# Reciprocals by Ln and Exp, and rows reversed by a transfer, in a fused linear-attention and state-space kernel

## The chip, the cores and the metric

The kernel runs on one core of a Trainium2 chip. A core has five engines that run side by side, each with its own in-order instruction queue: TensorE (PE, matrix products; PEld is its weight load), VectorE (DVE), ScalarE (ACT, which evaluates functions from a loaded table), GpSimd (POOL) and SyncE (SP), from which nearly all transfers of this kernel are issued. The engines wait for each other with semaphores. The metric is the device time of one execution in microseconds; a median of several runs is given.

## What is computed

Two independent parts, whose results stand side by side in one output of 2048 x 896.

Part A is linear attention with 16 heads of 28 over 2048 rows, whose features are softmaxes of a projection and of its negative:

```python
phi_q = concatenate([softmax(pq), softmax(-pq)])     # pk and phi_k alike
kv  = einsum("bhsf,bhsd->bhfd", phi_k, v)
z   = einsum("bhsf->bhf", phi_k)
num = einsum("bhqf,bhfd->bhqd", phi_q, kv)
den = einsum("bhqf,bhf->bhq", phi_q, z)[..., None] + 1e-6
o   = (num / den) @ wo
```

Part B convolves each of 448 columns of u (2048 rows) with a kernel that a diagonal state-space model with 256 states defines:

```python
P = exp(dt * A * l)                       # l = 0 .. 2047, A complex
K = einsum("dn,dnl,dn->dl", C, P, dt * B).real
y = irfft(rfft(pad(u)) * rfft(pad(K)))[:L] + u * Dskip
```

## The kernel before

Every operation is first recorded by a helper as a closure with its engine (`prog.add`), in the order of the code, and then issued in the order of a list of numbers, `ORDER` (1034 of them). So the program's text gives the numbers, and `ORDER` alone gives the order on each engine. Three more lists go with it: `PLACES` gives each buffer its place in one large SBUF tile `sbuf`, so buffers share bytes when their lives don't meet; `SLOTS` gives each product its PSUM banks; `PICKS` says for each copy, scaling or square (`copy`, `scaled`, `square`, lines 209, 212, 215) whether ACT or DVE does it: 228 letters, 17 of them V. Because of the helpers most instructions carry a helper's line: `mms` (L224) for products, `tt` (L181) for two-operand work on DVE, `af` (L202) for functions on ACT, `dma` (L244) and `dma_t` (L240, a transposing load) for transfers.

The stages, in the order in which they are recorded:

- Loads on SP: `log_dt`, the constants `PID` (six 128 x 128 matrices: the identity times 1, 3, 5, 7 and -1, and an anti-identity `REV`), six coefficient matrices of 224 KB (`load_raw`; one of them goes by ACT's queue), sixteen transposing loads of x (`load_x`), the weights, the DFT table `G1` (1 MB), and u.
- u is loaded by `load_u` (lines 274 to 276, with `row_pairs`, L267) in four transfers of 448 KB. A partition of the tile `ua[b]` holds pairs of neighbouring rows: index 0 of the pair is an even row and index 1 an odd row of u, 1792 contiguous bytes.
- Coefficients: step sizes on the diagonal (`DG`, and `DGN`, its negative by `scaled`), products with them, powers by Exp, cos and sin by Sin (`amp`, `cs`, `PW`), then `CB`, `K0`.
- `signal_spectrum(b)` (line 412) for the two halves b of u. The odd rows have to be in reversed order: four products per half with `REV` (L417, two recorded operations of two) give them in PSUM, two copies (L419) bring them to the tile `ur`; then a sum and a difference on DVE (L420, L421) give `ab`, and 64 products of 448 columns per half with `G1` (L434) give the spectrum, which goes to the DRAM tile `SUd`.
- `tables(qt)` for four quarters of the columns: angles by Sin (`rotations`), dampings by Exp (`dampings`), long products on DVE (`far`, `hi_tables`), 128 x 104 products in four column groups (`build_k`), and a rearrangement through the DRAM tile `KTd`.
- `key_side` (line 600) over eight pairs of row tiles: key features by Exp, their sums `bz` in PSUM, then a reciprocal on DVE (L620, `recip`, L198), written as bf16 into `VR`, and a multiplication of the values with it on DVE, which feeds the next products.
- `query_side(sc)` (line 637) over four row blocks: features, denominators, a reciprocal `R` (L664) of a 128 x 64 tile on DVE, a multiplication, a trip through the DRAM tile `SCd`, the output products and stores.
- `kernel_spectrum(qt)` and `conv(qt)`: products of spectra on DVE, inverse products on PE, eviction by ACT, stores.

Where two operations touch the same bytes (an SBUF place, a bank, a DRAM tile) the framework puts a semaphore wait in front of the second; a transfer's wait stands on the engine that issues it, and what is behind it on that engine's queue waits too. ACT's function tables are loaded by the compiler in front of an activation whose function the present table lacks.

Of the kernel before, what the change touches and what calls it, by code (L numbers as in the profile page):

```python
# [9 lines left out]
BF16 = mybir.dt.bfloat16  # L10
# [7 lines left out]
D_MODEL = 448  # L18
# [33 lines left out]
def _dft_tables():  # L52
# [24 lines left out]
    pid = np.zeros((128, 6, 128))  # L77
    for i, p in enumerate(ODD + [-1]):
        pid[np.arange(128), i, np.arange(128)] = p
    pid[np.arange(128), 5, 127 - np.arange(128)] = 1.0  # L80
# [43 lines left out]
def kernel(  # L124
# [23 lines left out]
    KTd = dram.tile([4, 3, 128, D_MODEL], BF16, name="KTd")  # L148
    SCd = dram.tile([4, 128, 128], BF16, name="SCd")
# [36 lines left out]
    def add(o, a, b):  # L186
        tt(o, a, b, ALU.add)
# [7 lines left out]
    def recip(o, a):  # L195
        def fn():
            with nc.allow_low_precision(reason="bf16 softmax weights, as in the reference"):
                nc.vector.reciprocal(o, a)  # L198
        prog.add("V", fn)

    def af(o, a, fn, **kw):
        prog.add("A", lambda: nc.scalar.activation(o, a, fn, **kw))  # L202
# [39 lines left out]
    def dma(eng, o, i):  # L242
        e = {"S": nc.sync, "G": nc.gpsimd}[eng]
        prog.add(eng, lambda: e.dma_start(out=o, in_=i))  # L244

    PID = sb([128, 6, 128])
# [3 lines left out]
    REV = PID[:, 5, :]  # L250
# [16 lines left out]
    def row_pairs(row, a):  # L267
        rs = u2.ap[0][0]
        return bass.AP(tensor=u2.tensor, offset=u2[row + 128 * (1 - a), 0].offset,
                       ap=[[2 * rs, 64], [256 * rs, 4], [1, 2 * D_MODEL]])  # L270

    ua = [sb([128, 4, 2, D_MODEL]) for _ in range(2)]

    def load_u(b):
        for a in range(2):
            dma("S", ua[b][64 * a:64 * a + 64].rearrange("p t r d -> p t (r d)"), row_pairs(1024 * b, a))
# [28 lines left out]
    dma("S", G1, G_d)  # L305
    load_u(0)
# [105 lines left out]
    def signal_spectrum(b):  # L412
        ab = sb([128, 2, 4, D_MODEL])
        ur = sb([128, 4, D_MODEL])
        for tp in range(2):
            bs = prog.banks(2)
            mms([(psum[:, bs[k], 0:D_MODEL], REV, ua[b][:, 3 - 2 * tp - k, 1, :], dict(start=True, stop=True))  # L417
                 for k in range(2)])
            copy(ur[:, 2 * tp:2 * tp + 2, :], two(bs))  # L419
        add(ab[:, 0], ua[b][:, :, 0, :], ur)  # L420
        sub(ab[:, 1], ua[b][:, :, 0, :], ur)  # L421
# [178 lines left out]
    def key_side():  # L600
        bK = prog.banks(1), prog.banks(1)
        for pr in range(8):
# [17 lines left out]
            recip(VR[:, :, :, D_HEAD, :], psum[:, bz, 0:64].rearrange("p (t s h) -> p t s h", t=2, s=2))  # L620
# [16 lines left out]
    def query_side(sc):  # L637
# [26 lines left out]
        recip(R, zz)  # L664
# [213 lines left out]
).split()]  # L878
PLACES = [64 * int(i) for i in (
# [52 lines left out]
```

## Time and profile before

| | |
|---|---|
| median of 3 runs | 236.51 us (236.47 to 238.96) |
| the profiled execution: its time, its span | 238.8 us, 237.1 us |
| instructions of PE, DVE, ACT | 3087, 263, 347 |
| table loads on ACT | 8 |
| transfers of u by `load_u` | 4 of 448 KB, issued from 5.25 us on |
| data moved by DMA | 36.99 MB in 82240 packets |
| granted clock of TensorE, mean | 0.985 |

A span reaches from the first to the last instruction; the execution's own time has a little more around it. Busy times are the time in which an engine has an instruction at work; matmuls are pipelined and their ends are modelled, so PE's is only rough. The idle time before an instruction is put down to what released it. The DMA share is the busy time of packets on the core's 16 DMA engines, as a share of all 16; packets that overlap on one engine can bring it above 1.

### The profile page before, as it was taken

To read this page: it belongs to the slowest core of one execution; us is meant where nothing else is said; L and a number is where in the kernel's file an instruction comes from. 1 tells how busy PE (TensorE), PEld (TensorE's weight loads), DVE (VectorE), ACT (ScalarE), POOL (GpSimd) and SP (SyncE) were. 2 spreads that over 40 slices of the span, in tenths; PEclk is the share of its full clock that TensorE was granted. 3 is DMA by queue.
4 is the path that set the end of the run, shared out by engine and by line. 5 is a ranking of instruction groups with operands and counts; after the bars stand their busy time and mean duration, and the time that the engine had idled before them with its cause. 6 is when DMAs were issued, how large, how long until landed. Compare 5 with 4: busy or idle time off the path is not lost.

```text
span 237.1 us, 7240 instructions
## 1 busy us (share of the span) xinstructions
PE 206.1 (87%) x3087; PEld 151.0 (64%) x3094; DVE 207.4 (87%) x263; ACT 191.7 (81%) x347; POOL 6.5 (3%) x21
## 2 busy tenths in 40 slices
PE   1448889999999899999999878499999969999991
PEld 1334435656548546687867867455579958779991
DVE  1899999999997799999999977589999996898950
ACT  3999999999999799999999999289756815935522
POOL 2000000000000100002000000000000000000000
PEclk9999999999999999999999999799999997999999
DMA  6999921849347786758266859907854990489395
GB/s 155 227 206 313 255 47 49 235 81 266 116 96 134 88 191 146 148 74 205 80 133 105 208 144 264 215 17 158 196 198 124 184 278 12 81 174 203 74 244 118
DMA packets 82240, 36.99 MB, mean 156 GB/s; under 512 B 65440, under 2 KB 80288, under 8 KB 81824
## 3 DMA queue, kind: packets, MB, share of 16 engines
q1 hardware_dynamic: 81968, 36.30, 70.4%
q8 instruction: 24, 0.39, 0.7%
q10 hardware_dynamic: 240, 0.23, 0.3%
q14 instruction: 8, 0.07, 0.1%
HBM read 20.04 MB, written 8.62 MB: 121 GB/s over the span
## 4 chain that ended last, share of the span: by engine, by line
PE 57%; ACT 6%; issue 5%; DMA 4%; DVE 4%; SPq 3%; ACTq 0%; POOL 0%; DVEq 0%; POOLq 0%
PE psum L224 57%; DVE sbuf L181 4%; ACT sbuf L209 3%; DMA sbuf<-SCd 3%; ACT sbuf L202 2%; SPq L244 2%; DMA out_dram<-sbuf 2%; SPq L240 1%; ACT sbuf L212 0%; ACT sbuf L215 0%; ACTq L927 0%; DVE sbuf L198 0%; PE psum L234 0%; POOL sbuf L219 0%; DVE sbuf L193 0%
## 5 line engine op out<-in xcount | busy, mean ns | idle before, releaser
L224 PE MATMUL psum<-sbuf 128*128 128x112 bf16 (+9 forms) x3051 | 204.7, 267 | 25.5 <-issue 6.8
L181 DVE TENSOR_TENSOR sbuf<-sbuf 128x896 bf16<-128x896 bf16 (+12 forms) x218 | 189.6, 936 | 16.6 <-ACT sbuf L202 4.4
L224 PEld LDWEIGHTS <-sbuf 128*128 128x128 bf16 (+4 forms) x3058 | 149.0, 116 | 79.8 <-issue 27.0
L209 ACT CAST sbuf<-psum 128x448 bf16<-128x448 f32 (+6 forms) x145 | 87.5, 675 | 29.5 <-PE psum L224 24.8
L202 ACT ACTIVATE sbuf<-psum 128x448 bf16<-128x448 f32 (+4 forms) x110 | 65.8, 755 | 0.0
L209 ACT COPY sbuf<-psum 128x192 f32<-128x192 f32 (+4 forms) x28 | 12.2, 470 | 6.1 <-PE psum L224 4.8
L215 ACT ACTIVATE sbuf<-sbuf 128x896 bf16<-128x896 bf16 (+1 forms) x16 | 16.5, 1098 | 0.7 <-DVE sbuf L181 0.7
L202 ACT ACTIVATE sbuf<-psum,sbuf 128x896 f32<-128x896 f32 (+3 forms) x17 | 13.3, 832 | 0.0
L202 ACT ACT_TABLE_LOAD x8 | 10.3, 1283 | 2.8 <-issue 1.5
L219 POOL MEMSET sbuf<- 128x224 bf16 (+6 forms) x16 | 6.0, 404 | 152.2 <-PE psum L224 142.0
L212 ACT ACTIVATE sbuf<-sbuf 128x896 bf16<-128x896 bf16 (+2 forms) x7 | 7.3, 1045 | 1.0 <-DVE sbuf L303 0.8
L209 ACT COPY sbuf<-sbuf 128x224 bf16<-128x224 bf16 (+2 forms) x14 | 7.3, 532 | 0.0
L198 DVE RECIPROCAL sbuf<-psum 128x64 bf16<-128x64 f32 x8 | 4.4, 552 | 2.1 <-ACT sbuf L209 1.9
L209 DVE CAST sbuf<-psum 128x448 bf16<-128x448 f32 (+1 forms) x5 | 4.0, 821 | 1.7 <-PE psum L224 1.7
L181 DVE TENSOR_TENSOR sbuf<-psum,sbuf 128x448 bf16<-128x448 f32 (+2 forms) x10 | 4.8, 498 | 0.6 <-ACT sbuf L209 0.6
L212 DVE TENSOR_SCALAR sbuf<-sbuf 128x896 bf16<-128x896 bf16 (+1 forms) x7 | 3.3, 490 | 0.0
L234 PE MATMUL psum<-sbuf 112*112 112x112 bf16 (+1 forms) x36 | 2.7, 216 | 0.4 <-DVE sbuf L181 0.4
L234 PEld LDWEIGHTS <-sbuf 112*112 112x112 bf16 (+1 forms) x36 | 2.4, 128 | 1.1 <-DVE sbuf L181 0.6
L198 DVE RECIPROCAL sbuf<-sbuf 128x64 f32<-128x64 f32 x4 | 2.2, 544 | 0.0
L193 DVE SCALAR_TENSOR_TENSOR sbuf<-sbuf 128x64 f32<-128x64 f32 (+1 forms) x5 | 1.9, 376 | 0.0
L209 ACT CAST sbuf<-sbuf 128x1792 bf16<-128x1792 f32 x1 | 1.8, 1793 | 0.0
L202 ACT ACTIVATE sbuf<-sbuf 112x4 bf16<-112x4 bf16 x1 | 0.2, 206 | 1.4 <-DMA sbuf<-in_B_log_dt_dram 1.4
(9 smaller groups left out, 3.4 us busy)
## 6 DMA issues: line engine op xcount, KB each, us to landing
sbuf<-SCd SPq DMA_DIRECT2D x16, 256.0 KB, 5.0
SUd<-sbuf SPq DMA_DIRECT2D x8, 448.0 KB, 3.9
sbuf<-SUd SPq DMA_DIRECT2D x4, 896.0 KB, 8.4
sbuf<-const SPq DMA_DIRECT2D x3, 1024.0 KB
sbuf<-const SPq DMA_DIRECT2D x8, 384.0 KB, 4.7
sbuf<-in_B_u_dram SPq DMA_DIRECT2D x4, 448.0 KB
out_dram<-sbuf SPq DMA_DIRECT2D x4, 448.0 KB, 4.1
out_dram<-sbuf SPq DMA_DIRECT2D x16, 112.0 KB, 3.7
```

Of the source, the lines that this page charges most:

```text
L181: prog.add("V", lambda: nc.vector.tensor_tensor(out=o, in0=a, in1=b, op=op))
L193: prog.add("V", lambda: nc.vector.scalar_tensor_tensor(out=o, in0=a, scalar=s, in1=b, op0=op0, op1=op1))
L198: nc.vector.reciprocal(o, a)
L202: prog.add("A", lambda: nc.scalar.activation(o, a, fn, **kw))
L209: either(lambda: nc.scalar.copy(o, a), lambda: nc.vector.tensor_copy(o, a))
L212: either(lambda: nc.scalar.activation(o, a, ACT.Copy, scale=s), lambda: nc.vector.tensor_scalar_mul(o, a, s))
L215: either(lambda: nc.scalar.activation(o, a, ACT.Square), lambda: nc.vector.tensor_tensor(out=o, in0=a, in1=a, op=ALU.mult))
L219: prog.add("G", lambda: nc.gpsimd.memset(o, v))
L224: nc.tensor.matmul(o, lhsT=l, rhs=r, **kw)
L234: nc.tensor.transpose(o, i, idn)
L240: prog.add("S", lambda: nc.sync.dma_start(out=o, in_=i, transpose=True))
L244: prog.add(eng, lambda: e.dma_start(out=o, in_=i))
```

## The change

Three parts, with all four lists made anew.

`recip` becomes two activations on ACT, the natural logarithm into a new F32 tile and then Exp with scale -1. It is called twelve times: eight in `key_side`, four in `query_side`. `af` now loads the table set `natural_log_exp_and_others` itself before the first Exp or Ln that follows a Sin (or nothing), so that one set serves both.

The anti-identity goes (`PID` has five matrices), and with it the eight products and the four copies of `signal_spectrum`. Instead one transfer, `reverse_u`, copies the odd rows of u in reversed order into a new DRAM tile `URd`, and `load_u` makes eight loads of 224 KB: the even rows from u into `ue`, the reversed odd rows from `URd` into `ur`.

`ORDER` has 1043 numbers, `PICKS` 224 letters, 26 of them V. SP's order begins: `log_dt`, five coefficient loads, `reverse_u`, the even rows of half 0 (two loads), `PID`, the first load of reversed rows of half 0, a part of `w_phi`, the second load, `G1`, then loads of x, the rest of u, the weights.

```diff
-    pid = np.zeros((128, 6, 128))
+    pid = np.zeros((128, 5, 128))
...
-    pid[np.arange(128), 5, 127 - np.arange(128)] = 1.0
...
+    URd = dram.tile([2, 512, D_MODEL], BF16, name="URd")
...
-    def recip(o, a):
-        def fn():
-            with nc.allow_low_precision(reason="bf16 softmax weights, as in the reference"):
-                nc.vector.reciprocal(o, a)
-        prog.add("V", fn)
+    def recip(o, a, t):
+        af(t, a, ACT.Ln)
+        af(o, t, ACT.Exp, scale=-1.0)
+
+    table = [None]
 
     def af(o, a, fn, **kw):
-        prog.add("A", lambda: nc.scalar.activation(o, a, fn, **kw))
+        def issue():
+            want = fn if fn == ACT.Sin else ACT.Exp
+            if want == ACT.Exp and table[0] != want:
+                nc.scalar.preload_act_table_set("natural_log_exp_and_others")
+            table[0] = want
+            nc.scalar.activation(o, a, fn, **kw)
+        prog.add("A", issue)
...
-    def row_pairs(row, a):
-        rs = u2.ap[0][0]
-        return bass.AP(tensor=u2.tensor, offset=u2[row + 128 * (1 - a), 0].offset,
-                       ap=[[2 * rs, 64], [256 * rs, 4], [1, 2 * D_MODEL]])
-
-    ua = [sb([128, 4, 2, D_MODEL]) for _ in range(2)]
+    ue = [sb([128, 4, D_MODEL]) for _ in range(2)]
+    ur = [sb([128, 4, D_MODEL]) for _ in range(2)]
+
+    def reverse_u():
+        rs = u2.ap[0][0]
+        dma("S", URd, bass.AP(tensor=u2.tensor, offset=u2[1023, 0].offset,
+                              ap=[[1024 * rs, 2], [-2 * rs, 512], [1, D_MODEL]]))
 
     def load_u(b):
         for a in range(2):
-            dma("S", ua[b][64 * a:64 * a + 64].rearrange("p t r d -> p t (r d)"), row_pairs(1024 * b, a))
+            rs = u2.ap[0][0]
+            dma("S", ue[b][64 * a:64 * a + 64],
+                bass.AP(tensor=u2.tensor, offset=u2[1024 * b + 128 * (1 - a), 0].offset,
+                        ap=[[2 * rs, 64], [256 * rs, 4], [1, D_MODEL]]))
+            dma("S", ur[b][64 * a:64 * a + 64],
+                URd[b].rearrange("(t z p) d -> z p t d", t=4, z=2)[1 - a])
...
     dma("S", G1, G_d)
+    reverse_u()
     load_u(0)
...
     def signal_spectrum(b):
         ab = sb([128, 2, 4, D_MODEL])
-        ur = sb([128, 4, D_MODEL])
-        for tp in range(2):
-            bs = prog.banks(2)
-            mms([(psum[:, bs[k], 0:D_MODEL], REV, ua[b][:, 3 - 2 * tp - k, 1, :], dict(start=True, stop=True))
-                 for k in range(2)])
-            copy(ur[:, 2 * tp:2 * tp + 2, :], two(bs))
-        add(ab[:, 0], ua[b][:, :, 0, :], ur)
-        sub(ab[:, 1], ua[b][:, :, 0, :], ur)
+        add(ab[:, 0], ue[b], ur[b])
+        sub(ab[:, 1], ue[b], ur[b])
...
-            recip(VR[:, :, :, D_HEAD, :], psum[:, bz, 0:64].rearrange("p (t s h) -> p t s h", t=2, s=2))
+            recip(VR[:, :, :, D_HEAD, :], psum[:, bz, 0:64].rearrange("p (t s h) -> p t s h", t=2, s=2),
+                  sb([128, 2, 2, 16], F32))
...
-        recip(R, zz)
+        recip(R, zz, sb([128, 4, 16], F32))
```

The lists `ORDER`, `PLACES`, `SLOTS` and `PICKS` are replaced as a whole.

More of the change, by code (lines that the diff above doesn't have):

```diff
@@ L244, in dma @@
         prog.add(eng, lambda: e.dma_start(out=o, in_=i))
-    PID = sb([128, 6, 128])
+    PID = sb([128, 5, 128])
     ident = PID[:, 0, :]
@@ L249 @@
     NEG = PID[:, 4, :]
-    REV = PID[:, 5, :]
     bias_hp = sb([128, 1], F32)
@@ L840 @@
 ORDER = [int(i) for i in (
[37 rows of a table removed]
[37 rows of a table added]
 ).split()]
 PLACES = [64 * int(i) for i in (
[12 rows of a table removed]
[12 rows of a table added]
 ).split()]
 SLOTS = [[int(c) for c in i] for i in (
[5 rows of a table removed]
[4 rows of a table added]
 ).split()]
 PICKS = (
-    "AVAVVVAAAAVVAAAAAAAVAAAAAAAAAAAAAAAAAAAAAAAVVAAVAAVAVVAAAAAAAAAAAAAAAAAAAAAAAAAVVAAAAAAAAAAAAAAAAAAA"
-    "AAAAAAAAAAAAAAAAAAAAAAAAAAAAAAAAAVAAAAAVAAAAAAAAAAAAAAAAAAAAAAAAAAAAAAAAAAAAAAAAAAAAAAAAAAAAAAAAAAAA"
-    "AAAAAAAAAAAAAAAAAAAAAAAAAAAA"
+    "VAVVVVAAAAVVAAAAVAAAAAAAAAAAAAAAAAAAAAAVVAAVAVVAVVVAAAAAAAAAAAAAAAAAAAAAAAAVVAAVAAAAAVAAAAAAAAAAAAAA"
+    "AAAAAAAAAAAAAAAAAAAAAAAAAAAAVVAAVAAVAAAAAAAAAAAAAAAAAAAAAAAAAAAAAAAAAAAAAAAAAAAAAVAAVAAAAAAAAAAAAAAA"
+    "AAAAAAAAAAAAAAAAAAAAAAAA"
 )
```

107 rows, old and new, of tables (ORDER, PLACES, SLOTS) are left out of this document.

## The prediction

> **What bounds the kernel now.** I read the page first: the busy shares, the DMA queues, then three stretches of the windows view.
>
> ```profile
> span 237.1 us, 7240 instructions
> ...
> PE 206.1 (87%) x3087; PEld 151.0 (64%) x3094; DVE 207.4 (87%) x263; ACT 191.7 (81%) x347; POOL 6.5 (3%) x21
> ```
>
> ```profile
> 0.00:17.73 17.73, 5.97 (x51) 4.67 (x52) 11.80 (x16) 13.91 (x18) 2.16 (x10) 1.00 0.94 196
> 17.73:228.40 210.67, 196.48 (x2967) 142.82 (x2973) 195.59 (x248) 176.36 (x328) 4.31 (x11) 0.98 0.70 152
> 228.40:237.10 8.70, 3.69 (x76) 3.53 (x72) 0.00 (x0) 1.40 (x3) 0.00 (x0) 0.98 0.72 160
> ```
>
> The third busy figure of a row is DVE. From 17.73 to 228.40 us it works 195.59 of 210.67 us, with 15.1 us idle. PE's 196.48 is as high, but its ends are modelled; the PE timeline has dense stretches like this one,
>
> ```profile
> 44.33 5.38 PE L224 MATMUL psum<-sbuf 128*128 128x448 bf16 x32
> ```
>
> 168 ns a matmul, where the group below has a mean of 357, so the records' lengths overstate PE and it has slack that its figure hides. After DVE's last instruction 8.7 us of inverse products, evictions and stores follow. I therefore count in DVE time: 17.73 + 195.6 + 15.1 + 8.7 = 237.1 us.
>
> ```profile
> 13.79 3.94 DVE L181 TENSOR_TENSOR sbuf<-sbuf 128x1792 bf16<-128x1792 f32 x2
> 17.92 10.90 DVE L181 TENSOR_TENSOR sbuf<-sbuf 128x1792 bf16<-128x1792 f32 x8 [0.18 <-ACT sbuf L202]
> ```
>
> These two rows of the DVE timeline end and begin at 17.73 and 17.92 us. It is the place that matters below: in the new order this is where DVE first asks for the reversed rows.
>
> **The change, term by term.** Prices come from these groups by form (busy us, mean ns).
>
> ```profile
> L198 DVE RECIPROCAL sbuf<-psum 128x64 bf16<-128x64 f32 x8 | 4.4, 552 | 2.1 <-ACT sbuf L209 1.9 <-PE psum L224 0.2
> L198 DVE RECIPROCAL sbuf<-sbuf 128x64 f32<-128x64 f32 x4 | 2.2, 544 | 0.0
> L209 DVE COPY sbuf<-sbuf 128x448 bf16<-128x448 bf16 x3 | 0.8, 273 | 0.0
> L212 DVE TENSOR_SCALAR sbuf<-sbuf 128x896 bf16<-128x896 bf16 x4 | 1.6, 393 | 0.0
> L216 DVE TENSOR_TENSOR sbuf<-sbuf 128x896 bf16<-128x896 bf16 x1 | 0.6, 632 | 0.0
> L209 DVE CAST sbuf<-psum 128x448 bf16<-128x448 f32 x3 | 1.8, 650 | 1.7 <-PE psum L224 1.7
> L209 DVE CAST sbuf<-psum 128x896 bf16<-128x896 f32 x2 | 2.2, 1077 | 0.0
> L209 ACT CAST sbuf<-psum 128x896 bf16<-128x896 f32 x25 | 22.8, 955 | 2.8 <-PE psum L224 2.8
> L212 ACT ACTIVATE sbuf<-sbuf 128x896 bf16<-128x896 bf16 x5 | 5.1, 1030 | 0.3 <-DVE sbuf L181 0.3
> L209 ACT COPY sbuf<-psum 128x128 bf16<-128x128 bf16 x4 | 1.3, 321 | 0.7 <-PE psum L234 0.7
> L202 ACT ACTIVATE sbuf<-sbuf 112x4 bf16<-112x4 bf16 x1 | 0.2, 206 | 1.4 <-DMA sbuf<-in_B_log_dt_dram 1.4
> L202 ACT ACT_TABLE_LOAD x8 | 10.3, 1283 | 2.8 <-issue 1.5 <-PEq L916 1.2
> L224 PE MATMUL psum<-sbuf 128*128 128x448 bf16 x392 | 80.3, 357 | 6.8 <-ACT sbuf L209 5.3 <-DVE sbuf L209 0.9 <-ACT sbuf L202 0.6
> ```
>
> Reciprocals: DVE loses 4.4 + 2.2 = 6.6 us. ACT gains 24 small activations; the trace has no Ln, so I bound one by the 4-element activation (206 ns) and the 128-element copy (321 ns): 5.0 to 7.7 us, taken as 6.4.
>
> Picks: read against the numbering of the operations, eleven jobs go from ACT to DVE and two the other way, with one eviction of equal form swapped. DVE gains three copies of 448 elements (0.8), the negated step matrix (0.3, as such a copy), two scalings of 896 (0.8), a square (0.6), a weight eviction (0.65) and two evictions of 320 elements (at most 2 x 0.65), and gives back one eviction of 896 (1.1): +3.4 us. With the reciprocals DVE stands at -3.2 us. On ACT the four evictions of reversed rows go (4 x 0.955 = 3.8 us) and the eleven jobs with them, two of which are 1.03 us each; it ends at or below its present sum and stays under DVE.
>
> Products: eight matmuls of 448 columns go, 8 x 0.168 = 1.3 to 8 x 0.357 = 2.9 us of PE, where PE works 5.97 of the first 17.73 us. Nothing of it is on the path while DVE is the fuller engine; if that cover went, 2.9 us is the most that it could return.
>
> Table loads: following the new order on ACT, Sin and the Exp/Ln group alternate eight times, as now; 8 x 1.283 us either way, cost nothing.
>
> The pair Ln, Exp stands in ACT's in-order queue, and the multiplication behind it on DVE waits for it. I summed ACT's and DVE's work in the new order up to each of the twelve places: the multiplication lies 0 to 6 us of DVE work behind the end of its Exp, so I cost it at nothing; its bound is the waits it replaces (2.1 us idle before RECIPROCAL) to twice them.
>
> The transfer: this is the large term. SP's order becomes: log_dt, five coefficient loads, the reversal, two loads of even rows, the constants PID, then the first load of reversed rows, one block of w_phi, the second load of reversed rows, the DFT table G1, and all of x and the weights. The first load of reversed rows reads what the reversal wrote to DRAM, so SP must stop there until that has landed, as it does today for another DRAM tile:
>
> ```profile
> SPq L244 <- DMA SCd<-sbuf: 5.1, 2, 3.6
> ```
>
> Behind it on SP stand G1, x and the weights. On DVE the first sum and difference of u stand after the same sixteen instructions that fill 11.80 us now, plus one of 0.3, so DVE reaches them at 18.0 us. PID's parts on the engines that the reversal holds queue behind it, so PE's next products (phases, K0) and ACT's eviction of K0 stop too. Nothing hides a late reversal.
>
> How late? Outermost, both access patterns count 2 (the halves of u); inside are 512 rows with a negative step, so the halves can't be joined. The two lines below (packets, MB, share of a queue; a transfer and its KB) show what one transfer does: 112 partitions by 2 rows are 224 packets, and the queue holds 240, 16 more, one closing packet for each engine. Sixteen divides 112: the split fits the outermost count.
>
> ```profile
> q10 hardware_dynamic: 240, 0.23, 0.3%
> ...
> sbuf<-in_B_A_re_dram ACTq DMA_DIRECT2D x1, 224.0 KB
> ```
>
> No transfer here has a small outermost count, so the trace gives two ends: all 16 engines, or one for each of the two halves. I take two, since the row nearest to it shows a split by the outermost count. The Trainium skill, page "DMA: Bandwidth & Descriptors", section "Why a DMA increments its semaphore by 16 and not by 1", has it as a rule: a transfer runs on the largest number of engines up to 16 that divides the outermost counts of both sides. By that rule it is two and the sum is the one below; against it, with 16, the sum is the faster rival's; nothing in this trace tests a count below 16.
>
> ```profile
> 2.00:4.00 2.00, 0.00 (x0) 0.00 (x0) 0.00 (x0) 0.61 (x2) 0.35 (x1) 1.00 0.72 208
> 4.00:6.00 2.00, 1.08 (x12) 1.08 (x13) 0.63 (x2) 0.85 (x3) 0.00 (x0) 1.00 1.11 261
> 6.00:8.00 2.00, 0.62 (x7) 0.37 (x5) 1.44 (x3) 2.00 (x4) 0.00 (x0) 1.00 1.09 261
> 20.00:22.00 2.00, 2.00 (x12) 1.42 (x11) 2.00 (x2) 2.00 (x4) 0.52 (x2) 1.00 0.94 393
> 40.00:42.00 2.00, 2.00 (x18) 1.27 (x17) 2.00 (x5) 1.99 (x2) 0.00 (x0) 1.00 0.72 236
> ```
>
> The last two figures are the busy share of 16 engines and GB/s. From 40 to 42 us the signal spectra go to DRAM in pieces of 896 bytes, the reversal's size: 236 / (16 x 0.72) = 20.5 GB/s for a busy engine, 43.7 ns a row. 512 rows on each of two engines take 22.4 us. Ends: 26.1 GB/s (20 to 22 us, long rows) gives 17.6 us, 14.7 GB/s (4 to 6 us, short rows from DRAM) 31.2 us. DRAM on both sides isn't in the trace; these ends are to hold it.
>
> It starts when the six coefficient loads (1.38 MB) have passed: by the first three rows that is 7.7 us. It lands at 7.7 + 22.4 + 1.5 = 31.6 us, the 1.5 my estimate of the part of a short transfer's 2.2 us (next fence) that comes after the last byte.
>
> ```profile
> KTd<-sbuf SPq DMA_DIRECT2D x4, 168.0 KB, 2.1
> KTd<-sbuf SPq DMA_DIRECT2D x4, 112.0 KB, 3.2
> ...
> sbuf<-KTd SPq DMA_DIRECT2D x16, 14.0 KB, 2.2
> ```
>
> ```profile
> 5.25 1.37 SPq L244 DMA_DIRECT2D sbuf<-in_B_u_dram  x2
> ...
> 30.74 0.95 SPq L244 DMA_DIRECT2D sbuf<-in_A_w_phi_dram  x2
> ```
>
> Then SP issues a load of reversed rows (1.37 / 2 = 0.69), w_phi (0.48) and the second load, which lands some 2.6 us later (between 2.1 and 3.2): 35.4 us. DVE waits 35.4 - 18.0 = 17.4 us, and everything after it moves along, because all engines were stopped by the same transfer.
>
> Sum: 35.4 + (195.6 - 3.2 - 0.3) + 15.1 + 8.7 = 251.3 us of span, +14.2. The profiled execution took 238.8 us for its span of 237.1; the median of the three runs shown is 236.51, 0.6 under that span. So I predict 251.3 - 0.6 = 250.7 us.
>
> **Rivals.** First, the other side: the reversal spreads over all 16 engines. Then it takes 917,504 bytes / (16 x 20.5 GB/s) = 2.8 us, lands at 12.0, the second load of reversed rows at 15.8, before DVE's 18.0. No wait, and DVE's -3.2 stands: 18.0 + 192.1 + 15.1 + 8.7 = 233.9, as a median 233.3 us. For it: the rates of the windows are those of 16 engines in every stretch. Against: the pattern's outermost 2. The point from which it decides: the reversal has to land by 31.6 - 17.4 = 14.2 us, so its rows have 14.2 - 7.7 - 1.5 = 5.0 us, which needs nine engines or more at 20.5 GB/s.
>
> Second, 16 engines, but the freed DVE time comes back as idle time, because PE sets the pace late in the run:
>
> ```profile
> 160.00:180.00 20.00, 20.00 (x194) 13.07 (x192) 19.87 (x20) 15.71 (x27) 0.00 (x0) 1.00 0.67 171
> ...
> 200.00:220.00 20.00, 20.00 (x374) 16.05 (x367) 17.57 (x19) 13.40 (x30) 0.00 (x0) 1.00 0.82 145
> ```
>
> Then only PE's 1.3 us are saved: 236.5 - 1.3 = 235.2 us.
>
> Third, the shared table isn't kept, and each Ln and each Exp loads its own: 24 x 1.283 = 30.8 us more on ACT; with the late reversal 281.5 us at most, and some 265 if half falls into ACT's idle time (210.67 - 176.36 = 34.3 us). For it only that the trace has no Ln; against it that the new code names one table for both.
>
> Fourth, the reversal is late but half of DVE's 15.1 us of idle time disappears, because ACT and PE stand ahead when DVE resumes: 243 us. That lies in the forecast's range.
>
> **Chances.** Two engines, with the wait: 0.80, by itself 240 to 262 us: the low end is the faster rate (-4.8) with some 6 us of idle time gained, the high end the slower rate (+8.8) with 2.5 us of worse waits. All 16 and faster 0.13; all 16 and no change 0.05; the table 0.02. The range 240 to 262 leaves out the other three, 2 in 10. A run of this kernel can tell about 1% (2.4 us) from no change: faster by more 0.13, within it 0.05, slower by more 0.82.
>
> **What would show it.** In the changed kernel: the DMA share near 2/16 = 0.12 from about 9 to 31 us, with some 40 GB/s; SP stopped at the first load of reversed rows until 30 us or later; DVE, PE and ACT idle together from about 18 to 35 us; RECIPROCAL gone, 24 more activations on ACT, eight table loads; DVE's busy sum near 204 us. I am wrong if the share stays near 0.7 or higher in that stretch and the first sum of u on DVE starts before 20 us; wrong in size only if the stop is there but the reversal takes outside 17.6 to 31.2 us.

## The result and the profile after

| | before | changed |
|---|---|---|
| median (range) | 237.74 us (236.47 to 240.28), 4 runs | 246.67 us (245.55 to 249.16), 4 runs |
| ratio | | 1.041, 95% interval 1.027 to 1.054 |
| profiled execution: time, span | 238.8, 237.1 us | 249.16, 247.4 us |

The changed kernel is slower, by about 9 us. A run more than 1.5% above the fastest of its kernel counts as slow; medians and ranges are of all runs, ratios of the fast ones alone, so a ratio can differ from the quotient of the medians. The changed kernel's profiled execution is the slowest of its four runs; the others have spans of 243.8 to 245.9 us.

The page's busy sums of the changed kernel, and its windows view cut where DVE stops and goes on (span of the window, then PE, PEld, DVE, ACT and POOL busy, the granted clock, the DMA share, GB/s):

```profile
span 247.4 us, 7239 instructions
...
PE 202.2 (82%) x3086; PEld 149.1 (60%) x3086; DVE 204.2 (83%) x260; ACT 186.7 (75%) x358; POOL 6.5 (3%) x21
```

```profile
0.00:17.60 17.60, 5.32 (x48) 4.47 (x48) 12.05 (x17) 13.26 (x16) 1.69 (x9) 1.00 0.37 106
17.60:32.97 15.37, 2.42 (x16) 1.91 (x16) 0.00 (x1) 2.04 (x4) 0.92 (x3) 1.00 0.44 125
32.97:236.82 203.85, 190.13 (x2937) 138.56 (x2938) 192.13 (x243) 169.38 (x336) 3.85 (x9) 0.99 0.76 158
236.82:247.40 10.58, 4.35 (x89) 4.19 (x86) 0.02 (x1) 1.98 (x5) 0.00 (x0) 0.89 0.69 175
```

DVE has 3.2 us less work than before (204.2 against 207.4), and the kernel is longer all the same: the second row is a hole of 15.37 us in which DVE does nothing and PE and ACT some 2 us each. In DVE time the four rows give 17.60 + 15.37 + 203.85 (192.13 busy, 11.72 idle) + 10.58 = 247.4 us.

What ends the hole is seen in the timelines of DVE, PE and ACT of the same run (start, us, engine, line, operation; in brackets the idle time before and what released it):

```profile
13.64 3.96 DVE L181 TENSOR_TENSOR sbuf<-sbuf 128x1792 f32<-128x1792 f32 x2
32.97 6.50 DVE L181 TENSOR_TENSOR sbuf<-sbuf 128x1792 bf16<-128x1792 bf16 x5 [15.37 <-DMA sbuf<-URd]
```

```profile
30.31 2.42 PE L230 MATMUL psum<-sbuf 128*128 128x224 bf16 x16 [15.07 <-DMA sbuf<-const]
```

```profile
32.77 0.53 ACT L215 CAST sbuf<-psum 128x448 bf16<-128x448 f32 x1 [13.33 <-PE psum L230]
```

DVE waits for the load of reversed rows, PE for the constants, ACT for PE. All three lead back to SP, whose timeline shows when it issued what:

```profile
3.74 0.81 SPq L250 DMA_DIRECT2D URd<-in_B_u_dram  x1
4.60 18.92 SPq L250 DMA_DIRECT2D sbuf<-in_B_u_dram  x2
...
28.06 0.59 SPq L250 DMA_DIRECT2D sbuf<-URd  x1
...
29.35 0.59 SPq L250 DMA_DIRECT2D sbuf<-URd  x1
```

The reversal is issued at 3.74, and the first load of its result only at 28.06 us. Between them SP was held twice: for 18.92 us while it issued the two loads of even rows (1.4 us in the kernel before), and then, after the constants at 23.56 us, by the wait for the reversal. The chain of waits puts it in one piece:

```profile
3.74 24.24 DMA URd<-in_B_u_dram
```

And this is what moved meanwhile, in windows of 2 us (the last two figures are the busy share of 16 DMA engines and GB/s):

```profile
8.00:10.00 2.00, 0.33 (x2) 0.17 (x3) 2.00 (x5) 2.00 (x4) 0.00 (x0) 1.00 0.14 45
...
20.00:22.00 2.00, 0.00 (x0) 0.00 (x0) 0.00 (x0) 0.00 (x0) 0.00 (x0) 1.00 0.14 45
...
24.00:26.00 2.00, 0.00 (x0) 0.00 (x0) 0.00 (x0) 0.00 (x0) 0.00 (x0) 1.00 1.00 279
```

From 8 to 22 us each window has a share of 0.14, close to 2 of 16 engines, and 44 to 45 GB/s. At 24 to 26 us, with the even rows and the constants under way, it is 1.00 and 279. If two engines move the 44.8 GB/s, each moves 22.4, which is 40 ns for a row of 896 bytes.

The other half of the change, in the groups by form of ACT:

```profile
L205 ACT ACT_TABLE_LOAD x4 | 5.1, 1283 | 1.3 <-PEq L922 1.3
L207 ACT ACT_TABLE_LOAD x4 | 5.1, 1283 | 0.1
L207 ACT ACTIVATE sbuf<-sbuf 128x64 bf16<-128x64 f32 x8 | 2.6, 346 | 0.0
L207 ACT ACTIVATE sbuf<-sbuf 128x64 f32<-128x64 f32 x8 | 2.5, 306 | 0.6 <-DVE sbuf L181 0.6
L207 ACT ACTIVATE sbuf<-psum 128x64 f32<-128x64 f32 x8 | 2.3, 288 | 0.0
```

Eight table loads as before, 24 activations of 64 elements for 7.4 us, and the group RECIPROCAL is gone from DVE.

### The profile page after: what moved, and what is told of

Its sections match the earlier page's. It is cut to its first block, busy times and chain, and to the rows that moved or that the text cites. A ratio compares the mean times of both kernels' runs of the same rounds, so it can differ in the third digit from the quotient of the medians.

```text
span 247.4 us, 7239 instructions
## 1 busy us (share of the span) xinstructions
PE 202.2 (82%) x3086; PEld 149.1 (60%) x3086; DVE 204.2 (83%) x260; ACT 186.7 (75%) x358; POOL 6.5 (3%) x21
## 4 chain that ended last, share of the span: by engine, by line
PE 39%; ACT 29%; DMA 15%; SPq 7%; issue 5%; DVE 3%; ACTq 0%; DVEq 0%
PE psum L230 38%; ACT sbuf L207 14%; ACT sbuf L215 11%; DMA URd<-in_B_u_dram 10%; SPq L250 5%; DVE sbuf L181 3%; DMA sbuf<-SCd 2%; ACT sbuf L221 2%; DMA sbuf<-in_A_x_dram 2%; SPq L246 1%; DMA sbuf<-KTd 1%; ACT L205 1%; ACT L207 1%; ACT sbuf L218 1%; PE psum L240 0%
## 5 line engine op out<-in xcount | busy, mean ns | idle before, releaser
L230 PE MATMUL psum<-sbuf 128*128 128x112 bf16 (+9 forms) x3050 | 201.0, 265 | 38.5 <-DMA sbuf<-const 18.1
L181 DVE TENSOR_TENSOR sbuf<-sbuf 128x896 bf16<-128x896 bf16 (+14 forms) x218 | 189.6, 936 | 27.6 <-DMA sbuf<-URd 15.4
L230 PEld LDWEIGHTS <-sbuf 128*128 128x128 bf16 (+4 forms) x3050 | 147.2, 115 | 90.9 <-issue 19.8
L215 ACT CAST sbuf<-psum 128x448 bf16<-128x448 f32 (+5 forms) x139 | 81.6, 648 | 40.3 <-PE psum L230 38.0
L207 ACT ACTIVATE sbuf<-psum 128x448 bf16<-128x448 f32 (+5 forms) x118 | 65.5, 676 | 1.8 <-PE psum L230 1.7
L221 ACT ACTIVATE sbuf<-sbuf 128x896 bf16<-128x896 bf16 (+1 forms) x15 | 15.4, 1055 | 0.7 <-DVE sbuf L181 0.7
L215 DVE CAST sbuf<-psum 128x448 bf16<-128x448 f32 (+4 forms) x7 | 4.5, 672 | 5.0 <-ACT sbuf L215 3.6
L207 ACT ACTIVATE sbuf<-sbuf 128x64 bf16<-128x64 f32 (+2 forms) x17 | 5.3, 319 | 2.0 <-DMA sbuf<-in_B_log_dt_dram 1.3
L215 ACT COPY sbuf<-sbuf 128x224 bf16<-128x224 bf16 (+2 forms) x11 | 4.8, 457 | 0.0
L218 ACT ACTIVATE sbuf<-sbuf 128x896 bf16<-128x896 bf16 (+1 forms) x4 | 4.4, 1096 | 0.5 <-DVE sbuf L181 0.5
L218 DVE TENSOR_SCALAR sbuf<-sbuf 128x896 bf16<-128x896 bf16 (+2 forms) x10 | 4.5, 447 | 0.0
```

The source lines that it names most:

```text
L181: prog.add("V", lambda: nc.vector.tensor_tensor(out=o, in0=a, in1=b, op=op))
L215: either(lambda: nc.scalar.copy(o, a), lambda: nc.vector.tensor_copy(o, a))
L218: either(lambda: nc.scalar.activation(o, a, ACT.Copy, scale=s), lambda: nc.vector.tensor_scalar_mul(o, a, s))
L221: either(lambda: nc.scalar.activation(o, a, ACT.Square), lambda: nc.vector.tensor_tensor(out=o, in0=a, in1=a, op=ALU.mult))
L230: nc.tensor.matmul(o, lhsT=l, rhs=r, **kw)
```

## The experiments

The theory: the reversal uses two engines because the outermost count of its patterns is 2, and its late landing is the whole loss; the Ln/Exp pair and the new lists together are a gain that it covers. A rival for the first: it is SP's being held, and with it the constants and the later loads, and not the reversed rows themselves. A rival for the second: the gain is from the new lists alone. All ratios are to the kernel before, run on the same chip in the same turns.

**The reversal on 16 and on 8 engines.** Only the outermost count is changed: 16 blocks of 64 rows in `URd`, or 8 of 128, and the loads read the blocks in the order that gives the same rows.

```diff
-    URd = dram.tile([2, 512, D_MODEL], BF16, name="URd")
+    URd = dram.tile([16, 64, D_MODEL], BF16, name="URd")
...
-        dma("S", URd, bass.AP(tensor=u2.tensor, offset=u2[1023, 0].offset,
-                              ap=[[1024 * rs, 2], [-2 * rs, 512], [1, D_MODEL]]))
+        dma("S", URd, bass.AP(tensor=u2.tensor, offset=u2[127, 0].offset,
+                              ap=[[128 * rs, 16], [-2 * rs, 64], [1, D_MODEL]]))
```

> The same reversal with an outermost count of 16 (blocks of 64 rows) instead of 2, everything else as in the changed kernel. Two-engine theory: 64 rows an engine at the 40 ns a row seen in the changed kernel are 2.6 us, so the reversal lands near 11 us, the second load of reversed rows near 16 us, DVE's wait of 15.4 us for URd is gone, and the time falls by 15.4 us from the changed kernel's 246.7 to about 231 us (230 to 234), ratio to before about 0.975. Rival, a copy from DRAM to DRAM with a negative step is slow by itself, whatever the engines: 45 GB/s stay, DVE waits to 33 us as now, 245 to 249 us. Second rival, the freed time comes back as idle time elsewhere on DVE: 235 to 238 us.

> The same reversal with an outermost count of 8 (blocks of 128 rows). Two-engine theory, that is, engines by the outermost count: DMA share near 8/16 = 0.5 and some 180 GB/s for about 5 us, landing near 14 us, the second load of reversed rows near 18.5 us, a DVE wait of 0 to 2 us, about 232 us (230 to 235). Rival, the copy is slow by itself: 245 to 249 us. Rival, any count other than 2 uses all 16 engines: share near 1 for 2.6 us.

Sixteen: 229.18 us, ratio 0.957 (0.949 to 0.964). Eight: 229.43 us, ratio 0.965 (0.958 to 0.971). Both are faster than the kernel before. With sixteen the wait for the reversed rows is gone; SP's timeline and the windows from DVE's view:

```profile
3.74 0.67 SPq L250 DMA_DIRECT2D URd<-in_B_u_dram  x1
4.45 1.38 SPq L250 DMA_DIRECT2D sbuf<-in_B_u_dram  x2
...
11.14 0.59 SPq L250 DMA_DIRECT2D sbuf<-URd  x1
```

```profile
0.00:17.45 17.45, 7.27 (x62) 6.14 (x63) 11.96 (x17) 13.17 (x16) 1.69 (x9) 1.00 0.85 250
17.45:217.24 199.79, 188.31 (x2937) 137.31 (x2942) 192.37 (x244) 171.14 (x339) 4.76 (x12) 0.99 0.74 159
217.24:227.80 10.56, 4.33 (x89) 4.17 (x85) 0.00 (x1) 1.96 (x5) 0.00 (x0) 0.90 0.69 175
```

With eight, SP's timeline, and the place in DVE's where it asks for the reversed rows:

```profile
3.73 0.85 SPq L250 DMA_DIRECT2D URd<-in_B_u_dram  x1
4.63 3.84 SPq L250 DMA_DIRECT2D sbuf<-in_B_u_dram  x2
...
13.12 0.59 SPq L250 DMA_DIRECT2D sbuf<-URd  x1
```

```profile
17.95 6.50 DVE L181 TENSOR_TENSOR sbuf<-sbuf 128x1792 bf16<-128x1792 bf16 x5 [0.42 <-DMA sbuf<-URd]
```

An engine has 64, 128 or 512 rows to move, and SP's first load of reversed rows starts at 11.14, 13.12 and 28.06 us. From 128 to 512 that is (28.06 - 13.12) / 384 = 38.9 ns a row, the 40 ns of the windows; from 64 to 128, where other loads keep the engines busy too, 31 ns. The time goes with the rows of one engine, and SP's hold at the even rows goes with them too: 1.38, 3.84, 18.92 us. Next to nothing is lost with eight engines: DVE waits 0.42 us. The share of 0.5 that was expected for them isn't seen (0.80 to 0.87 from 6 to 12 us), because coefficient loads and even rows run beside the reversal. The trace's record of each packet tells the engines apart better: rows of 896 bytes begin at 50 a us with the outermost count 2 (7 to 23 us), at 200 with 8 (7 to 8 and 10 to 12 us), and at 400 with 16 (7 to 9 us, even rows among them). That is 25 a us, or 40 ns a row, for each of 2, 8 and 16 engines. The expectations were 2 to 3 us too slow, since I had carried too much of DVE's idle time over from the kernel before: in the second window it is 199.79 - 192.37 = 7.4 us.

**The reversal on ACT's queue.** Two engines still; the transfer is issued by ACT behind its one coefficient load, so SP is free for the even rows and the constants. It runs beside the changed kernel as it is.

```diff
-    prog.add("S", lambda: nc.scalar.dma_start(
-        out=raw["Are"]...))
+    def are_and_reversal():
+        nc.scalar.dma_start(out=raw["Are"]...)
+        rs = u2.ap[0][0]
+        nc.scalar.dma_start(out=URd, in_=bass.AP(tensor=u2.tensor, offset=u2[1023, 0].offset,
+                                                 ap=[[1024 * rs, 2], [-2 * rs, 512], [1, D_MODEL]]))
+    prog.add("S", are_and_reversal)
```

> The changed kernel with the reversal on two engines still, but issued from ACT's queue right behind the one coefficient load that goes by that queue; SP issues everything else in the same order. Theory (the time is set by when the reversed rows arrive): the reversal lands at 24 to 28 us, since it is issued up to 2 us earlier at the most, DVE goes on at 31 to 33 us, and the time is 244 to 247 us, ratio about 1.03. Rival (what costs is SP, held for 18.9 us while it issued the loads of even rows behind the reversal, and with it the constants, G1 and x): those land early, K0 and the phases go on, and the time is 236 to 241 us.

> The changed kernel as it is, on the same chip as the other three, to be compared with them: 244 to 248 us, ratio 1.03 to 1.045, DMA share 0.14 from 8 to 22 us, SP held some 19 us at the loads of even rows, DVE waiting 15 us for the reversed rows.

On ACT's queue 248.56 us, ratio 1.039 (1.022 to 1.056); the changed kernel 244.39 us, ratio 1.032 (1.021 to 1.042). The intervals overlap: no gain. SP, ACT and DVE with the reversal on ACT's queue:

```profile
4.36 1.38 SPq L250 DMA_DIRECT2D sbuf<-in_B_u_dram  x2
5.78 0.61 SPq L250 DMA_DIRECT2D sbuf<-const  x1
29.31 0.59 SPq L250 DMA_DIRECT2D sbuf<-URd  x1
```

```profile
20.26 0.57 ACT L215 CAST sbuf<-psum 128x448 bf16<-128x448 f32 x1
```

```profile
34.01 6.50 DVE L181 TENSOR_TENSOR sbuf<-sbuf 128x1792 bf16<-128x1792 bf16 x5 [14.67 <-DMA sbuf<-URd]
```

SP isn't held any more, the constants are issued at 5.78 instead of 23.56 us, PE makes its sixteen products with them and ACT evicts the result at 20.26 instead of 32.77 us. None of it shortens the run, since DVE goes on at 34.01 us as it did at 32.97. So the rival falls as far as it rests on the even rows and the constants: the arrival of the reversed rows sets the time. G1 and x were no part of this test, since on SP they still stand behind the reversed rows (G1 is issued at 31.30 us). Nor were the clocks alike: TensorE's granted clock was 0.50 from 24 to 40 us here, where PE stood idle for 17.6 us, and 1.00 in the changed kernel. DVE's stretch behind the stop shows no cost of it: 201.40 us here, 200.52 in the changed kernel beside it. That the rows didn't arrive earlier was a small miss (24 to 28 us expected, first load at 29.31). The reversal now runs beside the coefficient loads, the even rows and the constants on the same two engines, which I take for the reason, though no run parts it off.

**Without the reversal.** Sixteen-block version, but the odd rows come straight from u.

```diff
-        dma("S", URd, ...)
+        prog.add("S", lambda: None)
...
-                bass.AP(tensor=URd.tensor, offset=URd[8 * b + 6 + a, 0, 0:1].offset,
-                        ap=[[D_MODEL, 64], [-128 * D_MODEL, 4], [1, D_MODEL]]))
+                bass.AP(tensor=u2.tensor, offset=u2[1024 * b + 128 * (1 - a) + 1, 0].offset,
+                        ap=[[2 * rs, 64], [256 * rs, 4], [1, D_MODEL]]))
```

> The changed kernel without the reversal: the odd rows are loaded straight from u in their own order, so the odd rows enter the spectrum unreversed; all else is as changed. Theory (a reversal on 16 engines is wholly hidden): as fast as the kernel with sixteen blocks within 1.5 us, 228 to 230 us, ratio about 0.957 to 0.965. Rival (the extra trip through DRAM and SP's wait for it still cost something at 16 engines): 2 to 5 us faster than that, 224 to 227 us.

228.08 us, ratio 0.961 (0.950 to 0.972), against 0.957 with the reversal on 16 engines: no difference that these intervals, about 1% either way, can tell. A reversal that lands in time costs nothing that can be measured here.

**Reciprocals back on DVE, in the new order.** The sixteen-block version, with each reciprocal on DVE at the place of the Ln, and nothing at the place of the Exp. Written that early, the reciprocals go into bytes that another tile still uses, so their values are not kept; instructions and sizes are the same.

```diff
-        af(t, a, ACT.Ln)
-        af(o, t, ACT.Exp, scale=-1.0)
+        def fn():
+            with nc.allow_low_precision(reason="bf16 softmax weights, as in the reference"):
+                nc.vector.reciprocal(o, a)
+        prog.add("V", fn)
+        prog.add("V", lambda: None)
```

> The sixteen-way reversal with the twelve reciprocals back on DVE, each at the place of its Ln in the order; the Exp's place stays empty. If DVE's time is what counts (the step by which I gave the reciprocals -6.6 us on DVE): 12 x 0.55 us more DVE time, so 5 to 7 us slower than the sixteen-way kernel, near 237 us. Rival, the reciprocals were hidden and ACT's 24 activations (7.4 us in the changed kernel) cost as much as DVE saves: within 2 us of the sixteen-way kernel.

235.70 us, ratio 0.992 (0.988 to 0.996). Its windows, cut in the same way:

```profile
0.00:17.45 17.45, 7.32 (x62) 6.19 (x63) 12.01 (x18) 13.21 (x16) 1.69 (x9) 1.00 0.90 255
17.45:222.90 205.45, 188.41 (x2936) 137.49 (x2940) 197.61 (x256) 168.81 (x315) 4.76 (x12) 0.99 0.70 154
222.90:233.40 10.50, 4.36 (x89) 4.20 (x86) 0.04 (x1) 1.99 (x5) 0.00 (x0) 0.82 0.69 176
```

Between 17.45 us and its end DVE has 197.61 - 192.37 = 5.2 us more work than with Ln and Exp and the same idle time (205.45 - 197.61 = 7.8 us), and the run is longer by 6.5 us between the medians, 5.6 between the profiled spans, and some 8 by the ratios (0.992 against 0.957). So in this order the pair on ACT is worth at least what it takes from DVE. The halved idle time (15.1 us before) comes with the lists, whichever engine makes the reciprocals; but they also give DVE more work and a longer tail, and by themselves, with the reversal, they are worth 0.8% (0.4 to 1.2). A list made for reciprocals on DVE might do better; that wasn't tried.

**Ln and Exp in the old order.** The kernel before, with nothing changed but the reciprocals: both activations at the old reciprocal's place, Ln written over its input, one table set for both.

```diff
     def recip(o, a):
         def fn():
...
-                nc.vector.reciprocal(o, a)
-        prog.add("V", fn)
+            activate(a, a, ACT.Ln)
+            activate(o, a, ACT.Exp, scale=-1.0)
+        prog.add("A", fn)
```

> The kernel before with only its reciprocals changed: at the place of each reciprocal in the old order stand Ln (in place, into the operand) and Exp on ACT, with the shared table; u is reversed by the anti-identity products as before. If DVE's time is what counts: 5 to 6.6 us less on DVE, 231 to 234 us against 237. Rival, in the old order the pair comes late in ACT's queue and DVE waits for it as long as it saves: 235 to 239 us. Rival, the shared table isn't kept: 24 more table loads of 1.28 us, above 250 us.

255.03 us (248.97 to 256.44), against 238.16 for the kernel before: a clear miss, and on the other side. Five of the six runs, the profiled one (256.44 us) among them, had a granted clock of 0.953 to 0.966; the sixth, at 0.991, took 248.97 us. So the loss is 10.8 us by that one run, at a clock like that of the kernel before, and 17 by the median. The table loads, and ACT's timeline in the stretch where DVE first waits for the pair:

```profile
L206 ACT ACT_TABLE_LOAD x7 | 9.0, 1283 | 1.3 <-PEq L925 1.2
L208 ACT ACT_TABLE_LOAD x7 | 9.0, 1283 | 0.1
```

```profile
74.09 1.28 ACT L208 ACT_TABLE_LOAD   x1
...
76.62 1.28 ACT L206 ACT_TABLE_LOAD   x1
77.92 0.21 ACT L208 ACTIVATE psum<-psum 128x64 f32<-128x64 f32 x1
78.16 0.22 ACT L208 ACTIVATE sbuf<-psum 128x64 bf16<-128x64 f32 x1
78.40 1.28 ACT L208 ACT_TABLE_LOAD   x1
...
84.25 1.28 ACT L206 ACT_TABLE_LOAD   x1
```

The old order puts reciprocals among the Sin functions, where they cost DVE 0.55 us and no table. On ACT such a place costs a load of the Exp/Ln table, 0.4 us of work, and a load back; with three such places there are 14 loads instead of 8. Does that explain the loss, or does the pair wait behind other work on ACT? To part the two, the same edit with two copies on ACT in place of Ln and Exp, which need no table:

```diff
-            activate(a, a, ACT.Ln)
-            activate(o, a, ACT.Exp, scale=-1.0)
+            nc.scalar.copy(a, a)
+            nc.scalar.copy(o, a)
```

> The kernel before, in its old order, with each of the twelve reciprocals replaced by two copies on ACT at the places that Ln and Exp had in the earlier run of the old order; it leaves the reciprocals out and multiplies with the sums instead. ACT has as many instructions as there, but no function that needs a table, so 8 table loads instead of 14. Theory (the 255 us of the old order with Ln and Exp came from the six more table loads and what waited for them): 232 to 240 us. Rival (the pair queues behind other work on ACT in an order not made for it): 245 to 252 us.

244.08 us, ratio 1.033 (1.019 to 1.046), between the two expectations: each theory has a part. There are eight table loads again,

```profile
L202 ACT ACT_TABLE_LOAD x8 | 10.3, 1283 | 1.4 <-PEq L916 1.2
```

and the 6 us above the kernel before are what 24 small jobs, and the waits for them, cost in an order not made for them. What Ln and Exp cost beyond the copies goes with the tables: 10.9 us between the medians (255.03 - 244.08), but 4.9 for the one run at 0.991 (248.97 - 244.08). For each of the six extra loads, of 1.28 us each, that is 0.8 to 1.8 us. DVE's waits for the two activations, and for the two copies, in the profiled runs (total, times, longest; the first line is that of all table functions, with the 4.1 us at the kernel's start in it):

```profile
DVE sbuf L181 <- ACT sbuf L208: 19.1, 10, 4.1
```

```profile
DVE sbuf L181 <- ACT sbuf L198: 5.6, 4, 2.1
```

In the windows from 70 to 90 us DVE is busy 12.42 us with Ln and Exp, 15.76 with copies and 16.81 in the kernel before. The rows in this order:

```profile
70.00:90.00 20.00, 14.17 (x298) 9.79 (x296) 12.42 (x9) 17.91 (x37) 0.97 (x3) 0.93 0.63 105
```

```profile
70.00:90.00 20.00, 17.29 (x322) 11.74 (x321) 15.76 (x13) 18.22 (x43) 0.97 (x3) 1.00 0.76 138
```

```profile
70.00:90.00 20.00, 18.97 (x340) 12.48 (x339) 16.81 (x16) 18.25 (x40) 0.97 (x3) 1.00 0.77 139
```

The first of them also had a lower granted clock (0.93, 0.95 over the run). How much of the 10.9 us is the clock's, and whether the holes in PE's work bring the lower clock, is open, so the tables' part is 5 to 11 us. Its direction is clearer: the fastest run with Ln and Exp (248.97) is slower than the slowest with copies (246.41), on chips on which the kernel before took 238.16 and 237.98 us.

## Why the prediction was right, step by step

The mechanism was the one predicted: the time is 246.67 us where 250.7 was forecast with 240 to 262 around it, and the sixteen-block run shows that without the late reversal the same kernel takes 229.18.

- **Two engines.** Right. The windows show a share of 0.14 and 45 GB/s, where 0.12 and 40 were named; with the outermost count alone changed to 8 and 16 the stop shrinks as the rows of one engine do. The Trainium skill, page "DMA: Bandwidth & Descriptors", section "Why a DMA increments its semaphore by 16 and not by 1", gives the rule that the largest number of engines up to 16 is taken that divides both outermost counts, and these three counts agree with it.
- **When it lands.** 31.6 us in the sum; SP went on at 28.06. Two terms were too long. One is the start: 512 rows of 40 ns are 20.5 us, which leaves 7.6 for start and landing together, where 7.7 + 1.5 = 9.2 had been counted. In the packet records the first reversed row begins at 6.18 us, while the last coefficient packets still run (to 7.04); it didn't wait for all of them. The other is the rate, 43.7 ns a row for a measured 40. What failed there is the division by the busy share: packets overlap on an engine (two engines show 0.14, not 0.125, and a row's packet takes 41 to 46 ns), so GB/s over 16 times the share gives too little for one engine. The same division on the reversal's own row, 45 / (16 x 0.14), gives 20.1 GB/s, where 22.4 were moved by each of two.
- **The wait.** DVE reached it at 17.60 (18.0 predicted) and went on at 32.97 (35.4): 15.4 us for 17.4. The second load of reversed rows was issued at 29.35 us and took 3.6 us from there, where 2.6 were predicted, which gives back a part of what the faster rate had saved.
- **What stops with it.** The stop of PE and ACT was right, its reason is only half of what happened. SP, held at the even rows, issued the constants no earlier than 23.56 us, which the prediction didn't have. After that they did queue behind the reversal on two engines: in the packet records 112 of their 128 packets have begun by 25.86 us and the other 16, the share of two engines, only between 28.13 and 28.90; PE starts at 30.31. On ACT's queue the reversal let them through. The Trainium skill, the same page, section "Queues, rings and completion order", says that a DMA engine takes packets in turn from the queues for which it has work; the run on ACT's queue agrees, with the constants in use before 20.26 us while the reversal went on past 28 us.
- **DVE's work.** -3.2 us predicted and measured; 192.1 us behind the stop predicted, 192.13 measured. That it fits so closely is partly luck. With the reciprocals back on DVE in the new order (the rows of that run above) DVE has 5.2 us more behind the first window, where 6.6 had been priced: the records of neighbouring DVE instructions overlap (in the kernel before a RECIPROCAL begins at 75.06 us and takes 0.56, the next instruction begins at 75.54), so durations add up to more than the time. And that run's sum, 209.7 us, is 2.3 above the kernel before, where the picks had been put at +3.4. Two misses of about 1 us cancel. ACT's 24 activations took 7.4 us for 6.4, within their bounds, and 8 table loads came as counted. The pair was hidden, as costed. In the waits of the sixteen-block run (total, times, longest) DVE waits for ACT's line of all table functions

```profile
DVE sbuf L181 <- ACT sbuf L207: 5.5, 3, 4.1
```

three times; the longest is the wait for the first Exp at the start, so what is left for the twelve pairs is at most 1.4 us.
- **Idle time and tail.** Carried over from before as 15.1 and 8.7 us, measured as 11.7 and 10.6. Here the sum was simply not worked out for the new lists. In the other profiled run of the changed kernel, the one beside the reversal on ACT's queue, the idle time was only 8.2 us,

```profile
33.32:233.84 200.52, 190.40 (x2938) 138.21 (x2939) 192.36 (x243) 168.86 (x335) 3.85 (x9) 0.99 0.75 161
```

so about half of it is gone, the effect of the fourth rival, though the sixteen-block run has it too, so it doesn't come from ACT and PE standing ahead after a stop. The tail of 10.4 to 10.7 us is in every run with the new lists; what lengthened it wasn't tried.

The sum against the profile: landing and loads -2.4, idle time -3.4, tail +1.9: 251.3 - 3.9 = 247.4 us, the measured span.

The first rival, 16 engines, was set at 233.3 us. Made real, it is 229.18: again the idle time (7.4 for 15.1), less the longer tail. Its deciding point, a landing by 14.2 us with nine engines or more, was near: with eight SP went on at 13.12 us, and DVE still waited 0.42, because the second load of reversed rows took 3.6 us from its issue (14.40 to 17.95) where 2.6 had been counted.

## What to carry to other kernels

Before a transfer replaces work on an engine, count the engines that it will use from the outermost counts of both patterns: two halves as the outermost dimension cost this kernel a wait of 15 us, and writing the same rows as 16 blocks made it faster than before by 4.3% (3.6 to 5.1). Moving a function to another engine is worth what the bound engine is freed of only if the order around it fits: Ln and Exp in the old order cost 11 to 17 us in place of a gain of some 6, partly for table loads between Sin functions and partly because the pair queues behind other work on ACT. And when a large loss sits in one wait, look for a gain that it covers, by removing the wait alone.

## What was not expected of the hardware

A transfer that keeps few engines busy for long also held the queue that issued it: SP needed 18.92 us to issue the next two loads, 3.84 with eight engines and 1.38 with sixteen, and with the reversal on ACT's queue it needed 1.38. Which limit was reached the runs don't show. And the same kernel's DVE idle time differed by 3.5 us from one profiled run to another (11.7 and 8.2 us), with one stop of 3.6 us behind an eviction of ACT in the longer one: that is the size of the spread between its runs.

```profile
L215 DVE CAST sbuf<-psum 128x240 bf16<-128x240 f32 x1 | 0.6, 586 | 3.6 <-ACT sbuf L215 3.6
```
